# Late attention scores on quarters of the array: two heads by two groups of 64 queries, plain float32, in place of float32r high and low parts

## The chip, the cores and the metric

One core of a Trainium2 chip runs the whole kernel in one launch. The metric is device time in microseconds (us) from the start to the end of an execution. The kernel before takes 660.93 us, the median of 3 runs (660.62 to 661.12). Engines are named as in the profile: PE is the matrix engine, PEld its weight loads, DVE, ACT and POOL the vector, scalar and GpSimd engines, SP the engine whose queue issues nearly all DMAs.

## The reference, cut to what matters

Attention with a band and ALiBi distances, and behind it a gated MLP without biases. There are 4 batches, 8 heads, 768 positions and a head size of 64; a query sees the first 8 keys and the 96 keys up to its own.

```python
scores = scale * np.matmul(q, k.transpose(0, 1, 3, 2))
dist = np.where(is_global & ~is_local, float(n_local), np.abs(rel).astype(np.float32))
scores = scores - slopes * dist
scores = np.where(is_global | is_local, scores, -1e9)
scores = scores - np.max(scores, axis=-1, keepdims=True)
a = np.exp(scores)
a = a / (np.sum(a, axis=-1, keepdims=True) + 1e-09)
x = np.matmul(a, v)          # then (B, S, H, D) -> (3072, 512)
h = x @ w_in                 # (3072, 512) @ (512, 2048)
g = h * np.clip(h + 3.0, 0.0, 6.0) / 6.0
out = g @ w_out              # (3072, 2048) @ (2048, 512)
```

Everything is float32, except that the two weight matrices come as 64-bit words from which the kernel decodes its float32 numbers.

## The kernel before, in words

**Tiling.** The 3072 tokens are 8 blocks of 384 (half a batch). A block needs 4 pairs of heads, so there are 32 pairs, n = 0 to 31, each with three tiles t of 128 queries. A product of the MLP is three float32r matmuls, since each operand is split in a high and a low part (`xh`/`xl`, `w1h`/`w1l`, `gh`/`gl`, `w2h`/`w2l`): line 168 is the first layer (12 matmuls of 384 columns for one of the 16 slices f of the hidden width, into a bank `hp`), line 200 the second (9 matmuls of 512 columns, into the three `acc` banks of the block). Between them stand the gates: ACT line 179 (`g`), DVE line 180, the high part `gh` on ACT (line 188) or POOL (line 186), and the low part `gl` on DVE (line 193).

**Stages.** The first 9 pairs (EARLY) are done ahead of the MLP, to about 59 us, with plain float32 scores (`scores` with `plain`, line 857): each head of the pair lies in one half of the array's rows, 64 rows by 128 columns, and each matmul runs as two passes. Their weights are transposed on PE (lines 904 and 906), copied to `pt` by ACT (line 908), and used in `values` (line 948). From 59 to 151 us slices of blocks 0 and 1 are mixed by the table ORDER, while ACT and DVE decode the MLP's weights (lines 376 to 427; the last decoded slice is f = 15). Then the rest of block 1 runs, with pairs 9 to 12 between its halves (stage "one", `rest_of_third`, to about 200 us), and from there the "layers": block i's MLP with the four pairs of block i+1 between its steps (`twos`, `attention`). Block 7 has no attention beside it and ends alone, from about 590 us.

**A late pair** (n = 9 to 31) goes through these steps before the change. `split`: q is scaled and split in `q1` (ACT, line 831) and `q2` (DVE, 835); `kx` holds a key's high part (POOL, 832) and low part (DVE, 838) in the two halves of 128 rows. `scores`, line 861: for each tile and head two float32r matmuls over all 128 rows, 232 keys wide (128 for the first tile of a batch). That is 12 matmuls a pair; in the layers those of tiles 0 and 1 stand at one place and those of tile 2 a unit later. `weigh`: a DVE pass (line 872) adds distances, keeps the least and frees the bank; ACT takes the exponentials (876). `normalize` (POOL, 896). `spread`: DVE transposes 32x32 blocks (921), and SP writes them to a DRAM tile `there`, one DMA for each tile (923). `fetch`: SP reads them back as the transposed `weights` with four DMAs (930), which wait for the writes to land. `values`: PE, 10 or 12 float32 matmuls of two passes, as 128 rows by 64 columns, one head in each half of the columns. `put_x` (ACT 154, DVE 155) writes the result as the next block's `xh` and `xl`. `values` of two pairs run together, at the end of every second pair.

**What sets the order.** `in_order` chains PE, SP and POOL to the order in which the program was written. DVE and ACT are ordered by the framework's scheduler, which may move an instruction ahead of others that were written before it. K and Q of a pair share one load (line 293), V has another; two rooms (`load_72`, `load_73`) are used in turn, so the load of pair n+2 waits for pair n. With `load_next` the K/Q load of n+2 is issued behind the last split of n.

Of the kernel before, what the change touches and what calls it, by code (L numbers as in the profile page):

```python
# [20 lines left out]
NT = 3  # L21
# [12 lines left out]
QW = 2 * TB  # L34
# [3 lines left out]
SLOPES = [2.0 ** (-8.0 * (h + 1) / H) for h in range(H)]  # L38
LEAST, MOST = (float(np.uint32(e << 20).view(np.float32)) for e in (896, 1151))
# [20 lines left out]
class Kernel:  # L60
# [162 lines left out]
    def attending(self, ctx, heads, rows, ps, **kw):  # L223

        if heads:
            self.hp = self.pool("hp", heads, ctx=ctx, **kw)
        self.up = self.pool("up", rows, ctx=ctx, **kw)
        self.tp = self.pool("tp", ps, ctx=ctx, **kw)

    def bank(self, what):  # L230

        s, t, x, o, h = ((self.ps_s, "sp"), (self.ps_t, "tp"), (self.ps_x, "xp"), (self.ps_o, "acc"), (self.ps_h, "hp"))
        pools = {"attention": {"s": (s, o, o, o), "t": (t, h, h), "x": (x,)}, "both": {"t": (t,), "x": (x,)},
                 "one": {"s": (o,), "x": (o,)}, "layers": {"s": (s, t), "t": (t,), "x": (x,)}}[self.stage][what]
# [45 lines left out]

    def rooms(self, pool, n, start=0):
# [6 lines left out]
    def load(self, n, values):  # L288

        if n < len(self.blocks) * NPAIR:  # L290
            end = KW + (TB if n < EARLY else QW)
# [12 lines left out]
    def loaded(self, n):  # L304
# [3 lines left out]
        q = at[:, KW:KW + QW].rearrange("p (j t c) -> p j t c", j=2, t=NT)  # L308
# [203 lines left out]
    def banded(self, flag):  # L512
# [12 lines left out]
        with ExitStack() as early, ExitStack() as words:  # L525
# [10 lines left out]
            with ExitStack() as ctx:  # L536
# [6 lines left out]
                self.attending(ctx, 0, 9, 5)  # L543
# [52 lines left out]
            self.weights()  # L596
            self.allowed = 4 * (2 * NF + 1)
# [9 lines left out]
        self.attending(self.ctx, 2, 3, 2, side="right")  # L607
        self.bp = self.pool("bp", 3, side="right")
        self.there = self.pool("there", 2, bass.MemoryType.DRAM)
# [39 lines left out]
    def rest_of_third(self, x, slices):  # L649
# [3 lines left out]
        for k in range(3):  # L653
            pairs[0].split(k, False)
        units[1] += [lambda: self.load_next(EARLY, False)]
        for p, (me, after) in enumerate(zip(pairs, pairs[1:])):
            at = units[4 * p + 1:]
            last = after is pairs[-1]
            at[0] += [lambda t=t, me=me: me.scores(t)() for t in range(NT)]
            at[1] += [me.sum_up] + [lambda t=t, me=me: me.normalize(t) for t in range(NT)]  # L660
            at[2] += [lambda t=t, me=me: me.spread(t) for t in range(NT)] + [me.fetch]
            for k in range(3):
                at[k + 3 if last else k].append(lambda k=k, after=after: after.split(k))
# [4 lines left out]
    def attention(self, i, x, first):  # L668
# [4 lines left out]
        for p in range(NPAIR):  # L673
# [11 lines left out]
            for t in range(1, NT if after else 0):  # L685
                at[t + 3].append(lambda t=t, after=after: after.split(t))
# [115 lines left out]
class Pair:  # L802
# [4 lines left out]
    def __init__(self, kernel, n, x, plain):  # L807
# [4 lines left out]
        self.parts = [{}, {}]  # L812

    def low(self, t):
        return CB if self.tb == 0 and t == 0 else 0

    def split(self, step, load=True):
# [3 lines left out]
        k, q, _, _ = kk.loaded(self.n)  # L821
        c = slice(CB if self.tb == 0 else 0, None)
        for j, part in enumerate(self.parts):
            h = 2 * self.pr + j
            scale = float(-1.0 / (np.sqrt(D) * SLOPES[h]))
            own, other = (slice(0, D), slice(D, P)) if j == 0 else (slice(D, P), slice(0, D))
            if step == 0:
                part["q1"] = kk.hp.tile([P, NT, P], F32R, name="q1")
                part["q2"] = kk.hp.tile([P, NT, P], F32R, name="q2")
                part["kx"] = kk.hp.tile([P, KW], F32R, name="kx")  # L830
                nc.scalar.mul(out=part["q1"], in_=q[:, j], mul=scale)
                nc.gpsimd.tensor_scalar(out=part["kx"][own, c], in0=k[own, c], scalar1=1.0, scalar2=0.0,  # L832
                                        op0=ALU.mult, op1=ALU.add)
            elif step == 1:
                nc.vector.scalar_tensor_tensor(out=part["q2"], in0=q[:, j], scalar=scale, in1=part["q1"].bitcast(F32),
                                               op0=ALU.mult, op1=ALU.subtract)
            else:
                nc.vector.tensor_tensor(out=part["kx"][other, c], in0=k[own, c], in1=part["kx"][own, c].bitcast(F32),  # L838
                                        op=ALU.subtract)
        if step == 2 and load:  # L840
            kk.load_next(self.n, False)

    def scores(self, t):
# [3 lines left out]
        if t != 1 or not self.plain:  # L847
            self.banks = [kk.bank("s")[:, 0:2 * W].rearrange("p (i c) -> p i c", i=2) for _ in range(2 if self.plain else 1)]
        sp = [self.banks[j][:, t % 2] if self.plain else self.banks[0][:, j] for j in range(2)]
# [4 lines left out]
        for j in range(2):  # L854
            if self.plain:
                rows = slice(j * D, (j + 1) * D)
                nc.tensor.matmul(sp[j][:, lo:W], lhsT=queries[rows, 0, t], rhs=keys[rows, c], start=True, stop=True)
            else:
                part = self.parts[j]
                for m, q in enumerate((part["q1"], part["q2"])):  # L860
                    nc.tensor.matmul(sp[j][:, lo:W], lhsT=q[:, t], rhs=part["kx"][:, c], start=(m == 0), stop=(m == 1))  # L861
        return lambda: self.weigh(t, sp, e, lo)

    def weigh(self, t, sp, e, lo):
        nc, kk = self.nc, self.k
        for j in range(2):
# [3 lines left out]
            else:  # L870
                d, scale = (kk.d0 if lo else kk.d1), SLOPES[h]
            nc.vector.tensor_tensor_reduce(out=e[:, j, lo:W], in0=sp[j][:, lo:W], in1=d, op0=ALU.add, op1=ALU.min, scale=scale,  # L872
                                           scalar=3.0e38, accum_out=self.least[:, i:i + 1])
        for j in range(2):
            i = 2 * t + j
            nc.scalar.activation(out=e[:, j, lo:W], in_=e[:, j, lo:W], func=AF.Exp, bias=self.least[:, i:i + 1], scale=-1.0,  # L876
# [12 lines left out]
    def normalize(self, t):  # L889
        nc, e, lo = self.nc, self.rows[t], self.low(t)  # L890
        for j in range(2):
            over = self.sums[:, 1, 2 * t + j:2 * t + j + 1]
            if self.n == 0:
                nc.vector.tensor_scalar(out=e[:, j, lo:W], in0=e[:, j, lo:W], scalar1=over, scalar2=None, op0=ALU.mult)
            else:
                nc.gpsimd.tensor_scalar(out=e[:, j, lo:W], in0=e[:, j, lo:W], scalar1=over, scalar2=0.0, op0=ALU.mult, op1=ALU.add)  # L896
# [14 lines left out]
    def spread(self, t):  # L911
# [3 lines left out]
        if t == 0:  # L915
            self.weights = kk.tp.tile([P, 4, NT, 2, 2, 32], F32, name="weights")
            self.there = kk.there.tile([P, 4, NT, 2, 2 * 32], F32, name="there")
        blocks = kk.bp.tile([P, 4, 2, 2, 32], F32, name="blocks")
        parts = slice(1 if self.low(t) else 0, None)
        for s, c in ((0, 0), (1, CB))[parts]:  # L920
            nc.vector.transpose(out=blocks[:, :, s].rearrange("p b j q -> p j b q"),  # L921
                                in_=e[:, :, c:c + P].rearrange("p j (b q) -> p j b q", b=4))
        nc.sync.dma_start(out=self.there[:, :, t, parts].rearrange("p b s c -> p b (s c)"),
                          in_=blocks[:, :, parts].rearrange("p b s j q -> p b (s j q)"))
# [103 lines left out]
```

## Time and profile before

| | before |
|---|---|
| median of 3 runs | 660.93 us (660.62 to 661.12) |
| the profiled execution, own time | 660.32 us |
| its span, start to end of the work in the trace | 658.5 us |
| PE busy | 647.1 us (98%) |
| DVE, ACT, POOL busy | 423.2, 286.4, 189.1 us |
| granted clock of PE | 1.00 in every stage |
| DMA engines busy, 206 to 590 us | 0.49 |

The profiled execution is 0.6 us below the median of the runs, and 1.8 us of it lie outside the span. Times in the trace count from the span's start. A row of the timeline gives start, duration, engine, line and operation; of a matmul the duration is longer than the step to the next, because matmuls overlap in the array, so costs on PE are read as differences of starts. A float32 matmul has two records, one for each pass, and a row with x20 holds 20 records.

### The profile page before, as it was taken

To read this page: it belongs to the slowest core of one execution; us is meant where nothing else is said; L and a number is where in the kernel's file an instruction comes from. 1 tells how busy PE (TensorE), PEld (TensorE's weight loads), DVE (VectorE), ACT (ScalarE), POOL (GpSimd) and SP (SyncE) were. 2 spreads that over 40 slices of the span, in tenths; PEclk is the share of its full clock that TensorE was granted. 3 is DMA by queue.
4 is the path that set the end of the run, shared out by engine and by line. 5 is a ranking of instruction groups with operands and counts; after the bars stand their busy time and mean duration, and the time that the engine had idled before them with its cause. 6 is when DMAs were issued, how large, how long until landed. Compare 5 with 4: busy or idle time off the path is not lost.

```text
span 658.5 us, 11444 instructions
## 1 busy us (share of the span) xinstructions
PE 647.1 (98%) x3933; PEld 581.0 (88%) x3933; DVE 423.2 (64%) x1147; ACT 286.4 (43%) x752; POOL 189.1 (29%) x377
## 2 busy tenths in 40 slices
PE   9989999999999999999999999999999999999997
PEld 7768899998989999999998999899899999989985
DVE  6888999998766876357654777356763676422222
ACT  6896877776333442244414333143331543121111
POOL 5663000002532433034241444124340342202100
PEclk9999999999999999999999999999999999999999
DMA  8676444432573675427552366615654275400001
GB/s 291 174 233 213 135 157 157 135 125 89 150 222 111 178 188 142 132 88 186 147 156 97 95 178 183 184 52 142 167 137 128 81 185 141 114 31 18 1 1 53
DMA packets 67316, 88.86 MB, mean 135 GB/s; under 512 B 10288, under 2 KB 52016, under 8 KB 67248
## 3 DMA queue, kind: packets, MB, share of 16 engines
q1 hardware_dynamic: 66960, 87.77, 45.9%
q8 instruction: 33, 0.54, 0.3%
q14 instruction: 35, 0.29, 0.1%
q10 hardware_dynamic: 288, 0.26, 0.1%
HBM read 65.08 MB, written 22.94 MB: 134 GB/s over the span
## 4 chain that ended last, share of the span: by engine, by line
PE 85%; DVE 9%; ACT 2%; issue 2%; POOL 1%; DMA 1%; POOLq 0%; DVEq 0%; ACTq 0%
PE hp L168 37%; PE acc L200 33%; PE xp L948 3%; PE sp L861 2%; PE tp L948 2%; PE tp L861 2%; PE sp L200 1%; DVE wz L423 1%; PE tp L200 1%; DVE wz L419 1%; PE xp L200 1%; DVE n L872 1%; ACT n L876 1%; DVE wz L411 1%; DVE g L180 1%
## 5 line engine op out<-in xcount | busy, mean ns | idle before, releaser
L179 ACT ACTIVATE g<-hp,small 128x384 f32<-128x384 f32 x127 | 73.6, 580 | 254.1 <-PE hp L168 147.2
L168 PE MATMUL hp<-xh,w1h 128*128 128x384 f32 x512 | 172.7, 337 | 0.4 <-ACT w1h L427 0.4
L168 PE MATMUL hp<-xh,w1l 128*128 128x384 f32 x512 | 172.3, 337 | 0.5 <-DVE w1l L416 0.5
L168 PE MATMUL hp<-xl,w1h 128*128 128x384 f32 x512 | 171.7, 335 | 0.0
L186 POOL TENSOR_SCALAR gh<-g 128x384 fp32r<-128x384 f32 x104 | 53.3, 512 | 289.1 <-DVE g L180 244.5
L180 DVE SCALAR_TENSOR_TENSOR g<-g,hp 128x384 f32<-128x384 f32 x128 | 70.2, 548 | 99.2 <-ACT g L179 98.8
L200 PE MATMUL acc<-w2h,gl 128*128 128x512 f32 x336 | 132.4, 394 | 0.2 <-DVE gl L193 0.2
L200 PE MATMUL acc<-w2h,gh 128*128 128x512 f32 x336 | 132.6, 395 | 0.0
L200 PE MATMUL acc<-w2l,gh 128*128 128x512 f32 x336 | 131.6, 392 | 0.0
L193 DVE TENSOR_TENSOR gl<-g,gh 128x384 fp32r<-128x384 f32 x128 | 75.9, 593 | 57.4 <-POOL gh L186 47.3
L896 POOL TENSOR_SCALAR n<-n,sums 128x232 f32<-128x232 f32 (+1 forms) x186 | 94.1, 522 | 48.4 <-DVE sums L887 42.5
L876 ACT ACTIVATE n<-n,least 128x232 f32<-128x232 f32 (+1 forms) x192 | 88.6, 464 | 30.4 <-DVE least L872 29.6
L168 PEld LDWEIGHTS hp<-xh,w1h 128*128 128x128 f32 x512 | 96.2, 188 | 3.4 <-ACT w1h L427 0.9
L168 PEld LDWEIGHTS hp<-xl,w1h 128*128 128x128 f32 x512 | 96.2, 188 | 2.1
L168 PEld LDWEIGHTS hp<-xh,w1l 128*128 128x128 f32 x512 | 96.0, 188 | 1.0 <-DVE w1l L416 0.8
L200 PEld LDWEIGHTS acc<-w2h,gl 128*128 128x128 f32 x336 | 63.0, 188 | 15.2 <-DVE gl L193 1.7
L200 PEld LDWEIGHTS acc<-w2h,gh 128*128 128x128 f32 x336 | 63.2, 188 | 13.3 <-issue 1.2
L200 PEld LDWEIGHTS acc<-w2l,gh 128*128 128x128 f32 x336 | 63.2, 188 | 11.6
L921 DVE STREAM_TRANSPOSE blocks<-n 128x256 f32<-128x256 f32 x127 | 49.4, 424 | 25.1 <-POOL n L896 23.1
L832 POOL TENSOR_SCALAR kx<-load 64x504 fp32r<-64x504 f32 (+1 forms) x46 | 29.1, 632 | 117.8 <-PE hp L168 96.1
L876 ACT ACTIVATION_READ_ACCUMULATOR n<-n,least 128x1 f32 x192 | 36.2, 188 | 0.0
L838 DVE TENSOR_TENSOR kx<-load,kx 64x504 fp32r<-64x504 f32 (+1 forms) x46 | 32.9, 715 | 1.8 <-POOL kx L832 0.4
(118 smaller groups left out, 731.5 us busy)
## 6 DMA issues: line engine op xcount, KB each, us to landing
wst<-w SPq DMA_DIRECT2D x32, 512.0 KB, 3.5
there<-blocks SPq DMA_DIRECT2D x58, 256.0 KB, 2.6
load<-pairs SPq DMA_DIRECT2D x23, 636.0 KB, 5.2
load<-pairs SPq DMA_DIRECT2D x32, 384.0 KB, 4.6
weights<-there SPq DMA_DIRECT2D x48, 192.0 KB, 3.6
weights<-there SPq DMA_DIRECT2D x44, 160.0 KB, 3.3
out<-o SPq DMA_DIRECT2D x23, 256.0 KB, 2.1
load<-pairs SPq DMA_DIRECT2D x8, 444.0 KB, 4.7
```

The costliest lines, as they stand in the source:

```text
L168: self.nc.tensor.matmul(hp, lhsT=self.w1(w, f)[:, kt, :], rhs=a[:, kt, :], start=(n == 0), stop=(n == 3 * NKT - 1))
L179: nc.scalar.activation(out=g, in_=hp, func=AF.Relu, bias=self.three, scale=1.0)
L180: nc.vector.scalar_tensor_tensor(out=g, in0=g, scalar=6.0, in1=hp, op0=ALU.min, op1=ALU.mult)
L186: self.nc.gpsimd.tensor_scalar(out=gh, in0=g, scalar1=1.0, scalar2=0.0, op0=ALU.mult, op1=ALU.add)
L193: self.nc.vector.tensor_tensor(out=gl, in0=g, in1=gh.bitcast(F32), op=ALU.subtract)
L200: self.nc.tensor.matmul(acc[tt], lhsT=a[:, tk], rhs=self.w2(w, f), start=(f == 0 and j == 0), stop=(f == NF - 1 and j == 2))
L832: nc.gpsimd.tensor_scalar(out=part["kx"][own, c], in0=k[own, c], scalar1=1.0, scalar2=0.0, op0=ALU.mult, op1=ALU.add)
L838: nc.vector.tensor_tensor(out=part["kx"][other, c], in0=k[own, c], in1=part["kx"][own, c].bitcast(F32), op=ALU.subtract)
L876: nc.scalar.activation(out=e[:, j, lo:W], in_=e[:, j, lo:W], func=AF.Exp, bias=self.least[:, i:i + 1], scale=-1.0, accum_out=self.sums[:, ...
L896: nc.gpsimd.tensor_scalar(out=e[:, j, lo:W], in0=e[:, j, lo:W], scalar1=over, scalar2=0.0, op0=ALU.mult, op1=ALU.add)
L921: nc.vector.transpose(out=blocks[:, :, s].rearrange("p b j q -> p j b q"), in_=e[:, :, c:c + P].rearrange("p j (b q) -> p j b q", b=4))
L948: nc.tensor.matmul(xps[j * D:(j + 1) * D, t * P:(t + 1) * P], lhsT=vt[0:K, t, j * D:(j + 1) * D], rhs=self.part(t, j, c, K), start=(c == 0 ...
```

## The change

Late pairs get plain float32 scores on quarters of the array. `packed` issues 12 matmuls: for each tile t, two groups g of 64 queries and two heads j, each 64 rows by 64 columns at position (64 j, 64 g), with only the 168 keys that a group of 64 queries can see (PW; before 232). A head has a bank of its own. All 12 stand at one place in program order, at the pair's first unit. There is no `split`: `scale` multiplies q in place by a column `over`, one ACT instruction a pair, emitted a few units ahead of the pair's scores.

```diff
+    def scale(self):
+        nc, kk = self.nc, self.k
+        _, q, _, _ = kk.loaded(self.n)
+        nc.scalar.mul(out=q, in_=q, mul=kk.over[:, self.pr:self.pr + 1])
+
+    def packed(self):
...
+        banks = [kk.bank(b)[:, 0:NT * PW].rearrange("p (t c) -> p t c", t=NT) for b in "st"]
+        keys, queries, _, _ = kk.loaded(self.n)
+        for t in range(NT):
+            for g in range(GROUPS):
+                own, c = slice(g * GQ, (g + 1) * GQ), t * TG + g * GQ
+                for j in range(2):
+                    rows = slice(j * D, (j + 1) * D)
+                    nc.tensor.matmul(banks[j][own, t], lhsT=queries[rows, t, own], rhs=keys[rows, c:c + PW], start=True, stop=True,
+                                     tile_position=(j * D, g * GQ))
+        for t in range(NT):
+            self.weigh(t, [bank[:, t] for bank in banks], kk.up.tile([P, 2, PW], F32, name="n"), 0)
...
-                for m, q in enumerate((part["q1"], part["q2"])):
-                    nc.tensor.matmul(sp[j][:, lo:W], lhsT=q[:, t], rhs=part["kx"][:, c], start=(m == 0), stop=(m == 1))
```

Everything behind the scores is 168 wide instead of 232. New masks `dl` and the column `over` are built on POOL behind the early stage (`packed_masks`). The way through DRAM changes: `there` has two fixed rooms with zeros written once (`zeros_ahead`); a pair writes it with two DMAs (64 queries each), both behind the pair's last transpose, where before each tile had its own; `fetch` needs eight DMAs instead of four, with runs of 768 bytes.

```diff
-        nc.sync.dma_start(out=self.there[:, :, t, parts].rearrange("p b s c -> p b (s c)"),
-                          in_=blocks[:, :, parts].rearrange("p b s j q -> p b (s j q)"))
+        if t == NT - 1:
+            for g in range(GROUPS):
+                own = slice(g * GQ, (g + 1) * GQ)
+                nc.sync.dma_start(out=kk.there[self.n % 2][own, :, g * SHIFT:g * SHIFT + 4],
+                                  in_=self.blocks[own].rearrange("p s b t j q -> p s b (t j q)"))
...
+        for s in range(2):
+            for b in range(4):
+                rows = NG if s == 1 and b == 3 else 32
+                nc.sync.dma_start(out=to[32 * b:32 * b + rows, :, s],
+                                  in_=there[:, s, b + (0 if s else AHEAD)].rearrange("(a p) c -> p a c", a=4)[0:rows])
```

Q is held once (QW is halved), so a late load of K and Q shrinks from 1272 to 888 columns, 636 to 444 KB. The load of pair n+2 stands directly behind the scores of n. In the layers the units now read:

```diff
-            for t in range(NT):
-                at[t].append(lambda t=t, me=me: me.scores(t)())
-            if after:
-                at[3].append(lambda after=after: after.split(0))
+            at[0] += [me.packed, lambda me=me: self.load_next(me.n, False)]
...
-            for t in range(1, NT if after else 0):
-                at[t + 3].append(lambda t=t, after=after: after.split(t))
+            if after:
+                at[4].append(after.scale)
```

**PE, the scores of pair 12** (the first pair inside the layers). Before: two tiles into the banks `sp` and `tp`, the third into `sp` again; `q1`, `q2` and `kx` carry the heads' numbers.

```order
L168 MATMUL hp<-xh,w1l_144 128x384
L861 MATMUL sp<-kx,q_2391 128x232
L861 MATMUL sp<-kx,q_2392 128x232
L861 MATMUL sp<-kx,q_2396 128x232
L861 MATMUL sp<-kx,q_2397 128x232
L861 MATMUL tp<-kx,q_2391 128x232
...
L861 MATMUL sp<-kx,q_2391 128x232
...
L168 MATMUL hp<-xh,w1h_143 128x384
```

After, at the same place, with `load_73` as the room of K and Q:

```order
L174 MATMUL hp<-xh,w1l_144 128x384
L865 MATMUL sp<-load_73 64x168
L865 MATMUL tp<-load_73 64x168
L865 MATMUL sp<-load_73 64x168
L865 MATMUL tp<-load_73 64x168
...
L174 MATMUL hp<-xh,w1h_143 128x384
```

The twelve matmuls now alternate between the two heads' banks, read q and k from the room itself, and the third tile no longer needs a bank that a DVE pass must free first.

**ACT, the end of the early stage.** Before: the last copies of transposed weights (`pt`) between casts of the MLP (`gh`, `xh`) and steps of the decoding (`wz`, `w1h`, `w2h`).

```order
L427 CAST w1h_143<-wz 128x4x128
L376 ACTIVATE wz<-wst 128x512
L188 CAST gh<-g 128x384
L908 COPY pt<-tp 128x512
L376 ACTIVATE wz<-wst 128x512
L154 CAST xh<-xp 128x384
L908 COPY pt<-tp 128x512
```

After, the same place:

```order
L461 CAST w1h_143<-wz 128x4x128
L410 ACTIVATE wz<-wst 128x512
L194 CAST gh<-g 128x384
L851 ACTIVATE load_72<-load_72,over 128x384
L851 ACTIVATE load_73<-load_73,over 128x384
L930 COPY pt<-tp 128x512
L410 ACTIVATE wz<-wst 128x512
L160 CAST xh<-xp 128x384
```

The scheduler has moved the scales of pairs 9 and 10, written for the stage "one", ahead of a `pt` copy of the early stage.

**SP, the way of pair 11 through DRAM.** Before: `load0_72` and `load1_73` are the two rooms, `there_2357` the pair's DRAM tile.

```order
L293 DMA load0_72<-pairs 128x1272
L293 DMA load0_72<-pairs 128x768
L923 DMA there_2357<-blocks_2358 512x1x64
L923 DMA there_2357<-blocks_2361 512x1x128
L923 DMA there_2357<-blocks_2365 512x1x128
L930 DMA weights_2356<-there_2357 32x4x320 x4
L293 DMA load1_73<-pairs 128x1272
```

After, with the fixed DRAM room `there1_1973`:

```order
L327 DMA load0_72<-pairs 128x888
L327 DMA load0_72<-pairs 128x768
L945 DMA there1_1973<-blocks_2336 128x1x768 x2
L956 DMA weights_2345<-there1_1973 32x4x192 x7
L956 DMA weights_2345<-there1_1973 8x4x192
L327 DMA load1_73<-pairs 128x768
```

Three writes, one for each tile as it is transposed, have become two that both wait for the last tile, and eight fetches stand where four stood.

More of the change, by code (lines that the diff above doesn't have):

```diff
@@ L279, in banded_masks, with packed_masks, zeros_ahead @@
         nc.gpsimd.tensor_copy(out=d1[:, PREV:CB], in_=glo)
+    def packed_masks(self):
+        c, ts = self.const, self.nc.gpsimd.tensor_scalar
+        self.dl = c.tile([P, 2, PW], F32, name="dl")
+        self.over = c.tile([P, NPAIR], F32, name="over")
+        for h in range(H):
+            self.nc.gpsimd.memset(self.over[h % 2 * D:(h % 2 + 1) * D, h // 2:h // 2 + 1], float(-1.0 / (np.sqrt(D) * SLOPES[h])))
+        self.nc.gpsimd.memset(self.dl[:, 0], FAR)
+        for g in range(GROUPS):
+            rows, start = slice(g * GQ, (g + 1) * GQ), g * GQ
+            for out, d in ((self.dl[rows, 0, CB - start:], self.d0[rows, 0:start + GQ]),
+                           (self.dl[rows, 1], self.d1[rows, start:start + PW])):
+                ts(out=out, in0=d, scalar1=1.0, scalar2=0.0, op0=ALU.mult, op1=ALU.add)
+    def zeros_ahead(self):
+        nc, pool = self.nc, self.pool("there", 1, bass.MemoryType.DRAM)
+        self.there = [pool.tile([P, 2, SPREAD, NT * 64], F32, name=f"there{i}") for i in range(2)]
+        zeros = self.bp.tile([P, 2, 4, NT, 2, 32], F32, name="blocks")[:, 0, 0:AHEAD].rearrange("p b t j q -> p b (t j q)")
+        nc.gpsimd.memset(zeros, 0.0)
+        for there in self.there:
+            for g in range(GROUPS):
+                own, k = slice(g * GQ, (g + 1) * GQ), g * SHIFT
+                if k > 0:
+                    nc.sync.dma_start(out=there[own, 1, 0:k], in_=zeros[own, 0:k])
+                if k < AHEAD:
+                    nc.sync.dma_start(out=there[own, 0, k + 4:], in_=zeros[own, k:])
     def rooms(self, pool, n, start=0):
@@ L811, in __init__, with first @@
         self.sums, self.rows, self.pts = None, [], []
-        self.parts = [{}, {}]
+        self.end = W if plain else PW
+    def first(self, t):
+        return self.tb == 0 and t == 0
     def low(self, t):
-        return CB if self.tb == 0 and t == 0 else 0
-    def split(self, step, load=True):
+        return CB if self.plain and self.first(t) else 0
+    def scale(self):
         nc, kk = self.nc, self.k
[L821 to L841, printed above, removed]
@@ L846, in scores @@
             self.sums = kk.up.tile([P, 2, 2 * NT], F32, name="sums")
-        if t != 1 or not self.plain:
-            self.banks = [kk.bank("s")[:, 0:2 * W].rearrange("p (i c) -> p i c", i=2) for _ in range(2 if self.plain else 1)]
-        sp = [self.banks[j][:, t % 2] if self.plain else self.banks[0][:, j] for j in range(2)]
+        if t != 1:
+            self.banks = [kk.bank("s")[:, 0:2 * W].rearrange("p (i c) -> p i c", i=2) for _ in range(2)]
+        sp = [self.banks[j][:, t % 2] for j in range(2)]
         e = kk.up.tile([P, 2, W], F32, name="n")
@@ L889, in normalize @@
     def normalize(self, t):
-        nc, e, lo = self.nc, self.rows[t], self.low(t)
+        nc, e, lo, end = self.nc, self.rows[t], self.low(t), self.end
         for j in range(2):
@@ L943, in values @@
         for t in range(NT):
-            two = not self.low(t)
+            two = not self.first(t)
             for c in range(2 if two else 1):
```

83 lines of the change are left out of this document (39 added, 44 removed).

## The prediction

> **What bounds the kernel now.** I read the busy times by stage first, then what PE waits for. In the stages, the columns are each engine's busy us (with its records), then the granted clock.
>
> ```profile
> 59.00:103.00 44.00, 43.96 (x234) 39.05 (x232) 41.77 (x85) 33.08 (x61) 0.00 (x0) 1.00 0.50 167
> 206.00:590.00 384.00, 384.00 (x2348) 350.06 (x2347) 233.94 (x640) 133.73 (x385) 124.69 (x239) 1.00 0.49 133
> ```
>
> From 206 to 590 us PE is busy 384.00 of 384.00 us; DVE, next, 233.94. What leaves PE's path there shortens the kernel one for one, and what leaves DVE, ACT or POOL is worth nothing unless PE waits for it. The change takes most of its work from those three (q2, kx, narrower passes), so I count that as zero. While the weights are decoded, from 59 to 103 us, DVE is busy 41.77 of 44 us and PE 43.96: two limits close together.
>
> **Removed on PE: the old scores.** The timeline of PE in the layers: one pair's tiles 0 and 1, then, one row later than the matmul at 309.87, its tile 2; the cost is the next start less the first.
>
> ```profile
> 305.08 0.56 PE L861 MATMUL sp<-kx,q 128*128 128x128 f32 x4
> 305.47 0.66 PE L861 MATMUL tp<-kx,q 128*128 128x232 f32 x4
> 305.96 0.40 PE L200 MATMUL acc<-w2h,gh 128*128 128x512 f32 x1
> ```
>
> ```profile
> 309.87 0.40 PE L200 MATMUL acc<-w2h,gl 128*128 128x512 f32 x1
> 310.11 0.60 PE L861 MATMUL sp<-kx,q 128*128 128x232 f32 x4
> 310.55 0.34 PE L168 MATMUL hp<-xh,w1h 128*128 128x384 f32 x1
> ```
>
> 0.88 + 0.44 = 1.32 us, and about 0.02 in the neighbours: 1.34 a pair. Pair 12 alone paid more, with the three tiles in one place:
>
> ```profile
> 203.12 0.60 PE L861 MATMUL sp<-kx,q 128*128 128x232 f32 x4
> ...
> 204.54 0.71 PE L861 MATMUL sp<-kx,q 128*128 128x232 f32 x4 [0.38 <-DVE least L872]
> 205.09 0.34 PE L168 MATMUL hp<-xh,w1h 128*128 128x384 f32 x1
> ```
>
> 1.97 us, since the third tile waited for a bank. The new form has both banks from the start, so 1.97 - 1.33 = 0.64 us go once.
>
> **Added on PE: the packed scores.** No quarter runs before, so I build the price from the two nearest forms. The early scores use row halves:
>
> ```profile
> 29.69 0.46 PE L857 MATMUL sp<-load 64*128 64x232 f32 x1
> 29.70 0.46 PE L857 MATMUL acc<-load 64*128 64x232 f32 x1
> 29.99 0.36 PE L857 MATMUL sp<-load 64*128 64x232 f32 x1
> 30.00 0.36 PE L857 MATMUL acc<-load 64*128 64x232 f32 x1
> 30.19 0.36 PE L857 MATMUL sp<-load 64*128 64x232 f32 x1
> ...
> 31.07 0.33 PE L904 MATMUL tp<-ident,n 128*128 128x128 f32 x1
> ```
>
> The two halves start 7 to 10 ns apart and share each step: 29.99 to 30.19 is one pass of both, 232 columns, 0.20 us (0.196 to the nanosecond). The late values use column halves, one head each:
>
> ```profile
> 314.40 0.33 PE L168 MATMUL hp<-xl,w1h 128*128 128x384 f32 x1
> 314.57 0.34 PE L168 MATMUL hp<-xh,w1l 128*128 128x384 f32 x1
> 314.84 1.32 PE L948 MATMUL xp<-weights,load 128*64 128x128 f32 x20
> 315.99 1.27 PE L948 MATMUL tp<-weights,load 128*64 128x128 f32 x20
> 317.19 0.50 PE L200 MATMUL acc<-w2h,gh 128*128 128x512 f32 x1
> 317.52 0.40 PE L200 MATMUL acc<-w2l,gh 128*128 128x512 f32 x1
> ```
>
> 40 records from 314.84 to 317.19, less about 0.16 at the ends, are 20 steps of two at 0.109 us for 128 columns. Between 128 columns (0.109) and 232 (0.196) the step grows by 0.84 ns a column, so 168 columns are 0.143 us (40 columns above the first). Row halves run together and column halves run together; if four quarters do both, 12 matmuls of two passes are 24/4 = 6 steps, 6 x 0.143 = 0.86 us.
>
> Each entry into tiles costs something: 314.57 to 314.84 is 0.27 where 314.40 to 314.57 is 0.17; the first step is about 0.05 longer, the last 0.11; 317.19 to 317.52 is 0.33 where 309.87 to 310.11 is 0.24. Together 0.10 + 0.05 + 0.11 + 0.09 = 0.35. A lower bound is what an early pair loses in itself: 31.07 - 29.69 = 1.38, less 6 x 0.196, is 0.20. I take 0.35, since the old row at full size stands on both sides here too. The old scores had no such cost; the new ones pay it once, having one place.
>
> Sum: 0.856 + 0.35 = 1.206 us a pair for 1.34, so 0.134 gained; over 23 pairs 3.1, and 3.7 with pair 12's 0.64. Against that stands a lag seen in one of the nine early pairs:
>
> ```profile
> 34.22 0.46 PE L857 MATMUL sp<-load 64*128 64x232 f32 x1
> 34.42 0.46 PE L857 MATMUL acc<-load 64*128 64x232 f32 x1
> ```
>
> Here the second half started a step late, and the pair took one step more. At one pair in nine, 23/9 x 0.143 = 0.4. PE gains **3.3 us**. Bounds: with the entry at 0.20, 23 x 0.15 = 3.5 more; if every pair lags a step, 23 x 0.143 = 3.3 less, which is nothing gained.
>
> **The scales of pairs 9 and 10 on ACT.** They now stand between a `gh` cast and the `pt` copy at the end of the early stage:
>
> ```profile
> 57.99 0.58 ACT L908 COPY pt<-tp 128x512 f32<-128x512 f32 x1
> ```
>
> ```profile
> 58.72 0.30 PE L904 MATMUL tp<-ident,n 128*128 128x128 f32 x1 [0.33 <-ACT pt L908]
> ```
>
> PE waits for this copy. Two scales of 128x384 have this row today, as q1:
>
> ```profile
> 153.55 0.93 ACT L831 ACTIVATE q<-load 128x384 fp32r<-128x384 f32 x2
> ```
>
> So PE starts up to 0.93 us late at 58.72. Part comes back where PE later waits for the decoded weights:
>
> ```profile
> 149.86 0.44 PE L168 MATMUL hp<-xh,w1h 128*128 128x384 f32 x1 [0.44 <-ACT w1h L427]
> ```
>
> ```profile
> 150.95 0.44 PE L168 MATMUL hp<-xh,w1l 128*128 128x384 f32 x1 [0.47 <-DVE w1l L416]
> ```
>
> 0.44 + 0.47 = 0.91 us of idle are there to take it, if the decoding does not slip too. It slips in part, since ACT also starts the next word (`wz`) late. Bounds 0 and 0.93; I take **0.5**. What q1 cost ACT later is gone, but ACT has room there.
>
> **Pair 11 through DRAM.** Before, the end of stage "one" on SP, then the start of pair 11's `values` on PE, then the landing times of all `weights` DMAs:
>
> ```profile
> 186.77 2.58 SPq L923 DMA_DIRECT2D there<-blocks  x3
> 192.23 1.76 SPq L930 DMA_DIRECT2D weights<-there  x4
> ```
>
> ```profile
> 197.60 0.66 PE L948 MATMUL acc<-weights,load 128*64 128x128 f32 x8
> ```
>
> ```profile
> DMA to landing us min/median/max: 2.6/3.5/4.9
> ```
>
> The last fetch is issued about 193.6 and lands 3.5 later, near 197.1: nothing is left before 197.60. Now both writes, 393 KB each, start behind the last transpose (about 188.8, when the third write was issued before), so they land about 0.6 later, near 192.8. Eight issues at 0.44 (1.76/4) put the last one at 192.8 + 7 x 0.44 = 195.9, landed between 2.6 and 3.5 later: 198.5 to 199.4. PE arrives near 197.6, 0.5 sooner by cheaper scores and 0.5 later by the scales. The scores of 12, then the MLP behind them, stand behind `values`. Cost 0.9 to 1.8, or 0 if the narrower passes bring the transposes a microsecond forward: I take **1.2**.
>
> **Pair 15.** The same race once more, in the layers:
>
> ```profile
> 261.91 1.92 SPq L930 DMA_DIRECT2D weights<-there  x4
> ```
>
> ```profile
> 267.60 0.95 PE L948 MATMUL tp<-weights,load 128*64 128x128 f32 x13
> ```
>
> 263.5 (the fourth issue) + 3.5 = 267.0, so no slack. Four more issues cost 1.8 us; against them, tile 2 gets its scores a unit earlier, and POOL has no kx ahead of the normalizing. But ACT's order has the scale of pair 17 one gate behind the exponentials of pair 15, and its load is issued only behind the eight fetches of 14; gates and PE queue behind a scale that waits. Bounds 0 and 2.5, I take **0.6**. What PE's weight loads wait for these DMAs in the whole kernel today (us, times):
>
> ```profile
>   DMA weights<-there: 0.5, 2
> ```
>
> So the other pairs have cover, and I count nothing there; where it went, a late fetch would cost up to 1.8.
>
> **The rest at nothing.** The masks on POOL come when it idles (0.00 busy from 59 to 103 us). The K/Q loads shrink by 192 KB. `zeros_ahead` is four writes before any late pair needs SP.
>
> **Sum.** -3.3 + 0.5 + 1.2 + 0.6 = -1.0. On the profiled execution that is 660.32 - 1.0 = 659.3 us, on the median, 0.6 above it, 660.93 - 1.0 = **659.9 us**. About 0.2%, 1.3 us, is what a measurement can tell from no change: this gain lies just inside, and I forecast no change that can be told.
>
> **The rivals.** *Gain without stalls.* If the narrower passes and missing kx bring the transposes forward by the 1.2 to 1.8 us that the fetches lose, and no pair lags, only the scales remain: -3.7 + 0.5 = -3.2, or 657.7, and 654.2 with the entry at 0.20. For it: POOL and DVE lose work just ahead of the transposes. Against: one DVE chain and one POOL chain per pair remain, and the writes have lost their early start.
>
> *Quarters run two at a time.* Then a pair is 12 x 0.143 + 0.35 = 2.07, 0.73 more than now, over 23 pairs 16.8, less pair 12's 0.6, and 2.3 of waits: 679. Milder, each group's weight loads hold up the other's matmul by half a step: 9 x 0.143 + 0.35 = 1.64, +6.9 - 0.6 + 2.3: 669.5. It decides from a step of about 0.17 us, where the gain is gone (1.34 - 0.35 over 6). Against it stand the 40 records of `values` in 2.35 us: with column halves in turn they would need 4.4. No row shows four quarters, so some chance stays. By the Trainium skill, "TensorE: Matmul & The Clock Gate", The mechanism, weight loads overlap matmuls in flight only when the row group differs, and each row group holds two of the quarters here: by that rule a pair would cost the 2.07, by the rows 1.21. The `values` rows disagree with the rule as far as it concerns column halves: their two heads share all row groups and still take one step together.
>
> *SP and ACT in every pair (slower).* A scale that waits for its K/Q load holds the gates on ACT, and PE behind them. The load stands behind eight issues, 3.4 us, where four took 1.8. If this costs 0.2 to 0.4 us in each of the 20 pairs of the layers, it is +4 to +8 less the 1.0 gained: 663.9 to 667.9. It decides from 0.12 us a pair ((1.0 + 1.3) / 20). Against: two gates stand ahead of the scale in the other blocks, and the load of n+2 is issued a pair ahead.
>
> **Chances.** Forecast 0.62, between 657.9 and 661.9 (the entry half way to 0.20 is -1.8, all three waits at their upper bounds would be +2.9, of which I grant two thirds; 0.26 of it faster by over 0.2%, 0.34 within, 0.02 slower); gain without stalls 0.16, all faster; quarters not together 0.09, slower; SP and ACT in every pair 0.13, slower but for 0.03. Faster 0.42, same 0.37, slower 0.21. The range reaches half way into the second case's cheap end and to the mild end of the last: 656.0 to 664.0.
>
> **What would show it.** Right: the twelve records of a pair's scores from first to next start take 1.2 us, four starts within about 30 ns; the `pt` copy is late by 0.9 and the waits of 149 to 151 us shrink; PE idles before the values of 11 and 15 for a `weights` DMA. Wrong: starts of quarters a step apart (second rival), ACT scales that wait for a DMA in most blocks (third), or no idle PE before `values` (first).

## The result, and the profile after

| | before | after |
|---|---|---|
| median | 660.79 us (4 runs, 660.62 to 661.12) | 671.77 us (4 runs, 671.07 to 674.05) |
| ratio, with 95% interval | | 1.0172 (1.0146 to 1.0197) |
| the profiled execution | 660.32 us | 674.05 us, the slowest of the four |
| its span, mean granted clock of PE | 658.5 us, 1.00 | 672.3 us, 0.992 |

The change makes the kernel 11.0 us slower; forecast was 659.9, and 664.0 was the upper end. First the new scores themselves. The timeline of PE, pair 12, with the first-layer matmuls on both sides:

```profile
207.62 0.34 PE L174 MATMUL hp<-xh,w1l 128*128 128x384 f32 x1
207.88 0.35 PE L865 MATMUL sp<-load 64*64 64x168 f32 x1
207.89 0.35 PE L865 MATMUL tp<-load 64*64 64x168 f32 x1
207.90 0.35 PE L865 MATMUL sp<-load 64*64 64x168 f32 x1
207.91 0.35 PE L865 MATMUL tp<-load 64*64 64x168 f32 x1
208.08 0.30 PE L865 MATMUL sp<-load 64*64 64x168 f32 x1
...
208.90 0.45 PE L174 MATMUL hp<-xh,w1h 128*128 128x384 f32 x1
209.18 0.34 PE L174 MATMUL hp<-xl,w1h 128*128 128x384 f32 x1
```

Four quarters start within 30 ns, and the next four 0.20 us later (0.14 in the steady steps). The twelve matmuls take 208.90 - 207.88 = 1.02 us; with 0.09 more at the entry (a step of 0.26 where 0.17 is usual) and 0.11 behind (0.28 for 0.17) that is 1.22 a pair where 1.21 was forecast. All 23 pairs read alike, with 1.01 or 1.02 us (pair 9 1.07) and no lag of a step. So the loss is elsewhere. Two stages after the change, and ahead of them the first of the two before it (the second stands in the prediction):

```profile
151.00:206.00 55.00, 54.62 (x334) 49.06 (x335) 37.61 (x111) 25.31 (x73) 18.74 (x36) 1.00 0.57 170
```

```profile
151.00:206.00 55.00, 51.97 (x345) 44.41 (x344) 26.22 (x86) 20.68 (x61) 12.61 (x27) 0.97 0.56 165
206.00:590.00 384.00, 376.50 (x2532) 332.39 (x2532) 179.63 (x577) 120.54 (x368) 92.59 (x199) 0.99 0.46 127
```

PE, busy in all of 384.00 us before, now stands idle for 7.5 of them, and for 3.0 in the stage of the pairs 9 to 11 (0.4 before); and its granted clock, 1.00 everywhere before, is 0.97 and 0.99. What PE waited for (total us, times, longest):

```profile
PE sp L974 <- DMA weights<-there: 4.0, 4, 1.5
PE hp L174 <- DVE g L186: 3.3, 2, 2.5
PE acc L974 <- DMA weights<-there: 3.0, 2, 2.2
...
PE tp L926 <- ACT pt L930: 1.7, 1, 1.7
```

Before, the `weights` DMAs cost PE next to nothing, no gate held it, and `pt` cost 0.3. New waits: 7.0 + 3.3 + 1.4 = 11.7, less 0.9 for the decoded weights that PE no longer waits for at 149 us. The clock: 672.3 x (1 - 0.992) = 5.4, nearly all of it in three stretches: behind the wait of pair 11, behind the gate in block 2 that follows here, and at the end of block 4. The scores: 23 x 0.12 + 0.64 = -3.4. That makes +12.8 of the 13.7 by which the two profiled executions differ; 0.9 is left unassigned.

The longest wait is in block 2, at the last pair. The timeline of all engines from 260 to 266.6 us, in part:

```profile
260.47 0.61 ACT L851 ACTIVATE load<-load,over 128x384 f32<-128x384 f32 x1 [7.84 <-DMA load<-pairs]
260.99 0.56 ACT L185 ACTIVATE g<-hp,small 128x384 f32<-128x384 f32 x1
261.58 0.55 DVE L186 SCALAR_TENSOR_TENSOR g<-g,hp 128x384 f32<-128x384 f32 x1 [7.08 <-ACT g L185]
262.19 0.44 PE L174 MATMUL hp<-xh,w1h 128*128 128x384 f32 x1 [2.49 <-DVE g L186]
262.32 0.51 POOL L192 TENSOR_SCALAR gh<-g 128x384 fp32r<-128x384 f32 x1 [8.41 <-DVE g L186]
...
262.82 2.71 POOL L918 TENSOR_SCALAR n<-n,sums 128x168 f32<-128x168 f32 x6
...
262.96 0.52 PE L174 MATMUL hp<-xh,w1h 128*128 128x384 f32 x1
263.28 0.52 PE L174 MATMUL hp<-xl,w1h 128*128 128x384 f32 x1
...
264.04 2.29 DVE L940 STREAM_TRANSPOSE blocks<-n 128x256 f32<-128x256 f32 x6 [0.61 <-POOL n L918]
```

ACT stood for 7.84 us at the scale of pair 17 until its K/Q load had landed; a gate that could have run stood behind it, DVE's part behind that, and PE. POOL, which takes its work in program order, had the same gate's `gh` ahead of the normalizing of pair 15, so the transposes of 15 began only at 264.04, although its last exponential had begun at 251.65. Soon after PE went on (262.96 to 263.28), a step took 0.32 us instead of 0.17: in the stretches around it the granted clock (the column behind the five engines) falls from 1.00 to 0.61.

```profile
258.00:262.00 4.00, 1.70 (x10) 1.38 (x8) 0.42 (x1) 1.08 (x2) 0.00 (x0) 1.00 0.38 116
262.00:265.00 3.00, 2.81 (x10) 2.81 (x11) 1.66 (x5) 0.58 (x1) 2.68 (x6) 0.61 0.00 0
```

Over the whole kernel, ACT's idle time ahead of a scale (us, times):

```profile
  DMA load<-pairs: 74.5, 17
```

In my theories below, **theory 1** is that the weights come late through DRAM, because of the writes and the eight fetches; **theory 2** that scales which the scheduler moved ahead wait on ACT and hold exponentials and gates; **theory 3** that a wait of PE also costs clock afterwards. Going in I held theory 1 to be the larger part.

### The profile page after: what moved, and what is told of

Read it like the earlier page. It is cut to its first block, busy times and chain, and to the rows that moved or that the text cites. A ratio compares the mean times of both kernels' runs of the same rounds, so it can differ in the third digit from the quotient of the medians.

```text
span 672.3 us, 11871 instructions
## 1 busy us (share of the span) xinstructions
PE 649.2 (97%) x4209; PEld 570.3 (85%) x4209; DVE 362.3 (54%) x1066; ACT 270.9 (40%) x729; POOL 154.7 (23%) x345
## 4 chain that ended last, share of the span: by engine, by line
PE 69%; DMA 10%; DVE 7%; ACT 4%; SPq 4%; POOL 3%; issue 3%; POOLq 0%; ACTq 0%; DVEq 0%
PE hp L174 30%; PE acc L206 29%; DMA there<-blocks 6%; SPq L956 4%; ACT n L898 3%; DMA load<-pairs 3%; DVE blocks L940 2%; PE sp L865 2%; PE xp L974 2%; POOL n L918 2%; PE sp L974 1%; DMA weights<-there 1%; DVE g L186 1%; PE sp L206 1%; PE xp L206 1%
## 5 line engine op out<-in xcount | busy, mean ns | idle before, releaser
L174 PE MATMUL hp<-xh,w1h 128*128 128x384 f32 x512 | 175.0, 342 | 3.3 <-DVE g L186 3.3
L206 PE MATMUL acc<-w2h,gh 128*128 128x512 f32 x336 | 134.0, 399 | 0.0
L199 DVE TENSOR_TENSOR gl<-g,gh 128x384 fp32r<-128x384 f32 x128 | 71.6, 559 | 68.4 <-POOL gh L192 58.3
L898 ACT ACTIVATE n<-n,least 128x168 f32<-128x168 f32 (+2 forms) x192 | 83.2, 435 | 60.6 <-DVE least L894 59.8
L174 PEld LDWEIGHTS hp<-xh,w1h 128*128 128x128 f32 x512 | 96.9, 189 | 10.4 <-DVE g L186 3.9
L918 POOL TENSOR_SCALAR n<-n,sums 128x168 f32<-128x168 f32 (+2 forms) x186 | 85.5, 476 | 42.9 <-DVE sums L909 23.8
L206 PEld LDWEIGHTS acc<-w2l,gh 128*128 128x128 f32 x336 | 63.6, 189 | 11.7
L940 DVE STREAM_TRANSPOSE blocks<-n 128x256 f32<-128x256 f32 x138 | 53.1, 424 | 25.5 <-POOL n L918 23.9
L851 ACT ACTIVATE load<-load,over 128x384 f32<-128x384 f32 x23 | 14.0, 614 | 74.5 <-DMA load<-pairs 74.5
L894 DVE CUSTOM_DVE_ANT_0 n<-sp,dl 128x168 f32<-128x168 f32 x60 | 19.6, 327 | 9.4 <-PE tp L865 9.3
```

The source lines that it names most:

```text
L174: self.nc.tensor.matmul(hp, lhsT=self.w1(w, f)[:, kt, :], rhs=a[:, kt, :], start=(n == 0), stop=(n == 3 * NKT - 1))
L199: self.nc.vector.tensor_tensor(out=gl, in0=g, in1=gh.bitcast(F32), op=ALU.subtract)
L206: self.nc.tensor.matmul(acc[tt], lhsT=a[:, tk], rhs=self.w2(w, f), start=(f == 0 and j == 0), stop=(f == NF - 1 and j == 2))
L894: nc.vector.tensor_tensor_reduce(out=e[:, j, lo:end], in0=sp[j][:, lo:end], in1=d, op0=ALU.add, op1=ALU.min, scale=scale, scalar=3.0e38, a ...
L898: nc.scalar.activation(out=e[:, j, lo:end], in_=e[:, j, lo:end], func=AF.Exp, bias=self.least[:, i:i + 1], scale=-1.0, accum_out=self.sums ...
L918: nc.gpsimd.tensor_scalar(out=e[:, j, lo:end], in0=e[:, j, lo:end], scalar1=over, scalar2=0.0, op0=ALU.mult, op1=ALU.add)
```

## The experiments

Each starts from the changed kernel. Medians are in us; the kernel before, on the same chip, had 660.82 beside e1 to e4, 660.91 beside e5 to e8, 661.16 beside e9 to e11 and 661.22 beside e12.

### e1, scales behind

```diff
+        before = [i.name for i in nc.cur_bb.bb.instructions if i.engine == mybir.EngineType.Activation][-1]
         nc.scalar.mul(out=q, in_=q, mul=kk.over[:, self.pr:self.pr + 1])
+        kk.tc.add_manual_dep(nc.cur_bb.bb.instructions[-1], before, mybir.DependencyInfo(
+            mybir.DependencyClass.NoSync, mybir.DependencyReason.DATA), reason="scale behind")
```

> Each scale keeps its written place on ACT, behind the ACT instructions written before it. Theory 1 (the weights come late through DRAM): only the copy of pt and a little of pair 11 are mended, so 670.0 to 671.5 us. Theory 2 (scales that wait on ACT hold exponentials and gates): the wait of 2.5 us for a gate goes with the slow clock behind it (1.5), the exponentials of 11 come 1 us sooner, and 0.6 net of the pt copy returns: 665.5 to 667.5. If the scores on quarters were the cause, nothing moves.

662.06 (ratio to before 1.0002, 0.9984 to 1.002): 9.7 us of the loss are gone, more than theory 2 expected. ACT no longer idles ahead of any scale. In the layers PE no longer waits for a `weights` DMA either; only pair 11 does:

```profile
PE acc L977 <- DMA weights<-there: 3.3, 2, 2.5
```

So most late weights were late because of ACT, and theory 1 falls as the root of the loss. SP's rows of pair 15, after and in e1, show it: the writes start 6.6 us sooner, while from there to the fetches it takes 5.1 in both.

```profile
266.36 1.16 SPq L945 DMA_DIRECT2D there<-blocks  x2
271.46 4.98 SPq L956 DMA_DIRECT2D weights<-there  x8
```

```profile
259.80 1.16 SPq L948 DMA_DIRECT2D there<-blocks  x2
264.90 3.53 SPq L959 DMA_DIRECT2D weights<-there  x8
```

### e2, four fetches

The rooms in DRAM keep both parts of a block side by side, so a fetch reads both.

```diff
-        self.there = [pool.tile([P, 2, SPREAD, NT * 64], F32, name=f"there{i}") for i in range(2)]
+        self.there = [pool.tile([P, 4, 2, NT * 64], F32, name=f"there{i}") for i in range(2)]
...
-            for g in range(GROUPS):
-                own = slice(g * GQ, (g + 1) * GQ)
-                nc.sync.dma_start(out=kk.there[self.n % 2][own, :, g * SHIFT:g * SHIFT + 4],
-                                  in_=self.blocks[own].rearrange("p s b t j q -> p s b (t j q)"))
+            for own, s, to, b in ((slice(0, GQ), 0, 0, 2), (slice(0, GQ), 1, 0, 0), (slice(GQ, P), 0, 0, 0), (slice(GQ, P), 1, 2, 0)):
+                n = 4 - max(to, b)
+                nc.sync.dma_start(out=kk.there[self.n % 2][own, to:to + n, s],
+                                  in_=self.blocks[own, s, b:b + n].rearrange("p b t j q -> p b (t j q)"))
...
-        for s in range(2):
-            for b in range(4):
...
+        for b in range(4):
+            nc.sync.dma_start(out=to[32 * b:32 * b + 32].rearrange("p a s c -> p a (s c)"),
+                              in_=there[:, b].rearrange("(a p) s c -> p a (s c)", a=4))
```

> The DRAM rooms hold both parts of a block side by side, so that four fetches with runs of 1536 bytes do what eight with 768 did; the writes become four with runs of 768 bytes, 0.59 MB instead of 0.79. Theory 1: four issues of 0.43 us less ahead of the last landing, minus two more writes at 0.5: each of the three late places gains about 1 to 1.7 us and part of its slow clock: 665 to 668 us. Theory 2: under 1.5 us of change, 670.3 to 672.

685.82 (1.0385, 1.0357 to 1.0413), far above either expectation, although the same way through DRAM is the shorter one in e5. ACT idled 77.9 us ahead of 16 scales here, and PE waited 10.4 us for weights in the layers:

```profile
PE sp L968 <- DMA weights<-there: 10.4, 4, 3.1
```

By itself this run tells nothing of the fetches: e5 shows that the same DMAs gain once the scales stay behind. Why the waits grew beyond the change's is not shown. One difference is on record: the K/Q loads, for which the scales wait, land in 4.7 us at the median here and in 3.3 in the change.

### e3, weights of the pair before

```diff
-        return self.weights[0:K, :, c, t, j]
+        return self.source[0:K, :, c, t, j]
...
+        if not self.plain:
+            self.source = kk.near if self.n % NPAIR == 3 else self.weights
+            kk.near = self.weights
```

> The values of every fourth pair (11, 15, ... 31) take the weights of the pair before, which landed long ago; all DMAs still run, but the output of those heads is not the reference's. It leaves out nothing but the wait. Theory 1: the waits for weights DMAs (7.0 us in the profile) go, with 2 to 3 us of slow clock behind them: 661.5 to 664 us. Theory 2: these waits are a consequence of late exponentials, but the wait of 2.5 us for a gate and the pt copy stay either way, so not below 661; above 668 would mean that the DRAM way is not the main cause.

663.1 (1.003, 1.0018 to 1.0042), inside theory 1's span. Taken alone it would have settled the matter for theory 1. But e1 gains as much without touching the DRAM way, so both take away the same waits, from two ends. What e3 leaves is the scale's own part:

```profile
PE hp L174 <- DVE g L186: 3.2, 2, 2.8
```

### e4, one unit earlier

```diff
-            at[3] += [me.sum_up, lambda me=me: me.normalize(0), lambda me=me: me.normalize(1)]
-            at[4] += [lambda me=me: me.normalize(2), lambda me=me: me.spread(0)]
-            at[5] += [lambda me=me: me.spread(1), lambda me=me: me.spread(2), me.fetch]
+            at[2] += [me.sum_up, lambda me=me: me.normalize(0), lambda me=me: me.normalize(1)]
+            at[3] += [lambda me=me: me.normalize(2), lambda me=me: me.spread(0)]
+            at[4] += [lambda me=me: me.spread(1), lambda me=me: me.spread(2), me.fetch]
```

> In the layers sums, normalizing, transposes and fetch stand one unit earlier (the scores of all tiles now stand at unit 0), about 2.5 us. Theory 1: the last pairs of blocks no longer wait (4.0 us in the profile, 2 to 3 of slow clock), pair 11 stays late: 665 to 667.5 us. Theory 2: the gate that waits behind a scale stays, with the pt copy: above 669. If POOL now holds up the gates by normalizing early, slower than 672.

671.44 (1.0146, 1.0116 to 1.0175): no gain. An earlier place in the program does not help work that waits on ACT. Theory 1, which expected 665 to 667.5, fails here. Theory 2 has the time right and one wait wrong: the gate that it expected to stay is no longer among PE's waits, while the waits for weights in the layers grew from 4.0 to 7.1 us; ACT still idled 57.5 us ahead of 16 scales.

### e5, scales behind and four fetches

The edits of e1 and e2 together.

> Scales behind, and the DRAM rooms of e2 (four writes, four fetches). If e2 was slow because its scales held ACT (its exponentials end long before the last transpose in six blocks), this is at or below 662: writes land 2.2 less after the last issue and two issues go, so pair 11 gains 1.5 to 2.5 us and some slow clock: 658.5 to 661. If e2 was slow because of the DMAs themselves, it stays above 670.

657.42 (0.9951, 0.9933 to 0.9969): faster than the kernel before by 3.5 us. SP's rows of pair 11, after and here:

```profile
190.31 1.16 SPq L945 DMA_DIRECT2D there<-blocks  x2
195.80 3.56 SPq L956 DMA_DIRECT2D weights<-there  x8
```

```profile
187.54 2.59 SPq L944 DMA_DIRECT2D there<-blocks  x4
191.93 2.26 SPq L953 DMA_DIRECT2D weights<-there  x4
```

From the end of the writes' issue to the first fetch it is 1.8 us here (191.93 less 187.54 + 2.59) and 4.3 after; four writes take longer to issue than two, so from the first write it is 4.4 and 5.5. And four fetches are issued in 2.26 instead of 3.56. PE still waits once, for 1.08 us, and its clock stays at 1.00 behind that.

```profile
198.25 1.32 PE L971 MATMUL acc<-weights,load 128*64 128x128 f32 x20 [1.08 <-DMA weights<-there]
```

### e6, scales behind and PE kept at work

```diff
+        any_, full = self.three.broadcast_to([P, P]), self.bank("s")
+        for _ in range(12):
+            self.nc.tensor.matmul(full[:, 0:P], lhsT=any_, rhs=any_, start=True, stop=True)
         pairs[-2].values("s")
```

> Scales behind, and 12 idle matmuls of 128 columns (2.6 us) on PE ahead of the values of pair 11, where PE waits 2.5 us for the weights; their result is not used. Theory 3 (a wait on PE of 2 us lowers the clock that it is granted for the next 3 to 4 us): the first layer behind the values goes at full clock again, 1.5 to 1.9 us less than e1, near 660.3. If the slow steps behind the wait come from something else (the DMAs, a cold start), the time stays at 662 or rises a little.

659.48 (0.9977, 0.9968 to 0.9987), 2.6 below e1; the two intervals only just touch, and the traces decide. The timeline of PE:

```profile
197.13 2.84 PE L655 MATMUL acc<-small 128*128 128x128 f32 x24
199.90 1.32 PE L980 MATMUL acc<-weights,load 128*64 128x128 f32 x20
201.14 0.44 PE L174 MATMUL hp<-xh,w1h 128*128 128x384 f32 x1
```

The values of 11 start no sooner than in e1 (199.90 here, 199.74 there). But the stretch behind them, first e1, then e6, has the clock at 0.57 there and at 1.00 here:

```profile
202.00:206.00 4.00, 4.00 (x16) 3.97 (x15) 0.56 (x1) 0.50 (x2) 0.00 (x0) 0.57 0.89 343
```

```profile
200.00:204.00 4.00, 4.00 (x36) 3.83 (x37) 0.56 (x1) 0.95 (x2) 0.00 (x0) 1.00 0.92 336
```

4 x (1 - 0.57) = 1.7 us are the clock's; most of the rest is a second wait of 0.82 in e1's values, which e6 does not have. Theory 3 holds here: the wait's price is the wait and the slow stretch behind it.

### e7, scales behind and one load later

```diff
-            at[0] += [me.packed, lambda me=me: self.load_next(me.n, False)]
+            at[0] += [me.packed]
+            at[2 if me.n == 11 else 0].append(lambda me=me: self.load_next(me.n, False))
...
-            at[2] += [lambda t=t, me=me: me.spread(t) for t in range(NT)] + [me.fetch, after.scale]
+            at[2][:0] = [lambda t=t, me=me: me.spread(t) for t in range(NT)] + [me.fetch]
+            at[2].append(after.scale)
```

> Scales behind, and the K/Q load of pair 13 behind pair 11's fetches in place of ahead of its writes. In e1 the writes of 11 took 6.8 us from the last issue to the first fetch, elsewhere 4.5. If 444 KB just ahead of them are why, 1 to 1.5 us less than e1 (and part of the slow clock): 659.5 to 661. If the writes are slow by themselves, no change: 662.

659.52 (0.9997, 0.9973 to 1.002; single runs from 658.51 to 664.42). Against e1 (0.9984 to 1.002) the times do not separate. SP's rows of pair 11 do, e1 first:

```profile
188.54 1.16 SPq L948 DMA_DIRECT2D there<-blocks  x2
195.91 3.56 SPq L959 DMA_DIRECT2D weights<-there  x8
```

```profile
188.03 1.16 SPq L950 DMA_DIRECT2D there<-blocks  x2
193.49 3.77 SPq L961 DMA_DIRECT2D weights<-there  x8
```

7.4 us from the first write to the first fetch in e1, 5.5 here: with the 444 KB of that load ahead of them, writes and landing took 1.9 us more.

### e8, scales behind and pairs closer together

```diff
-            at = units[4 * p + 1:]
+            at = units[3 * p + 1:]
```

> Scales behind, and pairs 9 to 11 three halves apart instead of four, so pair 11's scores, writes and fetches come two halves, about 5 us, earlier. If the late weights of 11 are all that is left of the loss (3.3 us of waits and about 1.8 of slow clock): 656.5 to 658.5, which beats both kernels. If the closer pairs collide on SP, POOL or ACT, the gain is partly lost: 659 to 662.

664.26 (1.0048, 1.003 to 1.0066), slower than e1. Pair 11 now waits for its V, whose load stands behind its own fetches on SP:

```profile
202.25 2.40 PE L977 MATMUL acc<-weights,load 128*64 128x128 f32 x20 [4.47 <-DMA load<-pairs]
```

I had only looked at the weights; the room for V comes free no sooner than before.

### e9 and e10, which scales

e9 keeps only the scales of pairs 9 and 10 in place, e10 only the others.

```diff
+        if self.n <= 10:
+            kk.tc.add_manual_dep(nc.cur_bb.bb.instructions[-1], before, mybir.DependencyInfo(
```

> Only the scales of pairs 9 and 10 keep their written place; the later ones may be moved ahead, as in the change. This leaves the pt copy free (0.6 net) and tells the price of the other scales: if these hold the loss (theory 2), 670 to 671.5 us, close to the change; if the late start at the pt copy shifts everything behind it into bad places, below 666.

> The other half: the scales of pairs 9 and 10 stay ahead of the pt copy, those of 11 to 31 keep their written place. Theory 2: close to e1, 662 plus 0.3 to 1 for the pt copy, 662.3 to 663.5 us. If the pt copy mattered more than its net 0.6, above 665.

e9: 673.93 (1.0203, 1.0171 to 1.0235), above what was expected. e10: 661.44 (1.0004, 0.9991 to 1.0018), a little below. The loss that e1 gives back lies with the scales of pairs 11 to 31. In e10 the `pt` copy is as late as in the change, and the time does not show it, since PE then finds the decoded weights ready (103 to 151 us, PE busy 47.93 of 48), and the scores of pair 9 start at 159.19, against 159.27 in e1:

```profile
PE tp L930 <- ACT pt L934: 1.7, 1, 1.7
```

```profile
103.00:151.00 48.00, 47.93 (x239) 42.67 (x238) 46.01 (x93) 36.25 (x65) 0.00 (x0) 1.00 0.42 132
```

### e11, e5 and the load later

The edits of e5 and e7 together.

> e5 with e7's move of one load: scales behind, four writes and four fetches, and the K/Q load of pair 13 behind the fetches of 11. e5 still waits 1.1 us for the weights of 11. If that load is in the way there too, about 1 us less than e5: 656.3 to 657. If nothing is in the way any more, 657.4.

657.68 (0.9949, 0.9933 to 0.9966): the same as e5. With four short writes the load is no longer what pair 11 waits for.

### e12, the load ahead of the fetches

The scales are free to move again; only the load's place on SP changes.

```diff
-            at[0] += [me.packed, lambda me=me: self.load_next(me.n, False)]
+            at[0] += [me.packed, lambda me=me: self.load_next(me.n, False)] + ([pairs[p - 1].fetch] if p > 0 else [])
...
-            at[5] += [lambda me=me: me.spread(1), lambda me=me: me.spread(2), me.fetch]
+            at[5] += [lambda me=me: me.spread(1), lambda me=me: me.spread(2)] + ([me.fetch] if p == NPAIR - 1 else [])
```

> The change with its scales as they were (free to be moved ahead), but in the layers the K/Q load of pair n+2 stands ahead of the fetches of n-1 on SP in place of behind them. If the scales wait because their load queues behind eight fetches that wait for writes, the 74.5 us of waiting on ACT shrink to under 40, the gate of block 2's end no longer holds PE for 2.5 us, and the last pairs of blocks have no late weights; pair 11 in the stage before is untouched (4 to 5 us with its slow clock): 662 to 665 us. If the scales' place on ACT alone decides, whatever the load does, it stays at 670 to 672.

665.03 (1.0052, 1.0034 to 1.0069). ACT's idle time ahead of the scales falls from 74.5 to 33.5 us:

```profile
  DMA load<-pairs: 33.5, 16
```

SP's rows around the load of pair 17, after and here, show its two places:

```profile
253.63 3.56 SPq L956 DMA_DIRECT2D weights<-there  x8
257.29 0.36 SPq L327 DMA_DIRECT2D load<-pairs  x1
```

```profile
251.23 0.33 SPq L327 DMA_DIRECT2D load<-pairs  x1
254.37 3.56 SPq L956 DMA_DIRECT2D weights<-there  x8
```

Six microseconds sooner, and the first layer no longer waits for a gate (0.4 us of such a wait is left, ahead of `values`). What is left over e5 is in the main pair 11, with 3.1 us of waits and a slow stretch behind them (the scores of 12 start at 208.47, in e5 at 203.86), and 1.5 us for weights in the layers. So in the layers the loss needs both: a load behind eight fetches that wait for writes, and an instruction on ACT that waits for it ahead of others that need not.

## Why the prediction was wrong, step by step

- **The packed scores: right.** 1.21 us a pair forecast, 1.22 measured; the four quarters run together. The lag that I charged (0.4 us) did not occur. No part of the loss is here: with the scales behind and the shorter DMAs, e5 gains 3.5 us by its medians, where the prediction's PE term was 3.3. The second rival is out, and so is its page's rule as the prediction read it: by the Trainium skill, "TensorE: Matmul & The Clock Gate", The mechanism, weight loads overlap matmuls in flight only when the row group differs. Here the two quarters of one row group (207.88 and 207.90, both `sp`) start within 20 ns, and from the second pass on all four follow every 0.14 us. The same section of the Trainium skill also lets a load into a background weight buffer run ahead, which the prediction left out.
- **The scales at the `pt` copy: right in mechanism, 0 in size.** The wait rose to 1.7 us, and all of it had come back by the scores of pair 9 (e10 against e1); I had charged 0.5.
- **Pair 11: mis-sized.** I charged 1.2 us. The waits were 3.0, and a slow stretch followed. Of the chain, the transposes were 1.5 us later than before (write at 190.31; I took 188.8 from before), since the exponentials stood behind the scale of 12; e1, without that, still waits 3.3, since the loads then stand directly ahead of the writes. The landing was the other miss: I put the first fetch at 192.8, it came at 195.80.
- **Pair 15, and the line "So the other pairs have cover, and I count nothing there": the step that failed.** I saw the scale one gate behind the exponentials, with its load behind the eight fetches of 14, and gave it 0.6 with an upper bound of 2.5. The gate alone was 2.5 with a slow stretch behind it, and the weights of 15 were late by another 1.9 (half of the 4.0 above; the other half is the end of block 4, where I had counted nothing, with 0.8 for a gate besides and a slow stretch again). The bound was too low because it counted the wait once: the gate that stands behind the scale feeds PE, and the normalizing of 15 stands behind that gate's `gh` on POOL, the transposes behind the normalizing.
- **The third rival was the one, and I argued it down.** "The load of n+2 is issued a pair ahead" is true of the program and false of the queue: SP reaches it only when the writes of n-1 have landed and eight fetches are issued (257.29, while the scores of 15 stood at 248). Seventeen scales waited. Most waits were covered, which is why the time rose by 11 us and not by 74.5; the price came at few places, not as 0.2 to 0.4 us in each pair as the rival had it.
- **Missing altogether: the clock.** Nothing in the trace of before shows PE idle for 2 us once it is busy, so the sum had no term for it. In the change the clock cost 5.4 us of the profiled execution, more than any single wait.

What stays open: 0.9 us of the profiled difference, why e2's waits grew, and how the gain of e5 over e1 (4.6 us) divides between the writes and the fetches, which were not tried apart.

## What to carry to other kernels

Where a scheduler may reorder an engine that runs in order, look in the changed order for every instruction that waits for a DMA, and hold its place on the engine against the time at which that DMA can be issued on its queue, not against its place in the program. Price a wait of the matrix engine with what stands behind the waiting instruction and, from about 2 us on here, with a likely slow stretch of the clock afterwards. And two experiments that each give back the same ten microseconds (e1 and e3) name one chain, not two causes: cut it at its start before mending its end.

## What the runs showed of the hardware

- After PE idled 2.5 us (e1, 199.74, with 0.82 more behind it) or 2.49 (after, 262.19), its granted clock was 0.57 and 0.61 in the next 3 to 4 us; after 1.08 us (e5) it stayed at 1.00, and with PE kept at work through the wait (e6) too. The Trainium skill, "TensorE: Matmul & The Clock Gate", HAM oscillation, gives as its rule no PE-idle gaps over about 3.4 us; here a single gap of 2.49 was enough. The size alone does not decide: in e2 a wait of 1.99 us (522.22) was followed by 0.70 over the next 4 us, and one of 2.29 (360.58) by 1.00.
- Fewer and longer runs did not make the writes to DRAM quicker. Two writes in runs of 3 KB landed later than three in runs of 512 bytes or four in runs of 768. Each of the two also carried more and came from 64 partitions, as the four did, where the three came from 128; no run separates these. From the DMA issues of the profile's page, with KB each and median us to landing, of before, after and e2 (its larger ones):

```profile
there<-blocks SPq DMA_DIRECT2D x58, 256.0 KB, 2.6
```

```profile
there<-blocks SPq DMA_DIRECT2D x46, 384.0 KB, 3.7
```

```profile
there<-blocks SPq DMA_DIRECT2D x46, 192.0 KB, 2.9
```
